# Mamba-2 scan and maxout FFN on one core: first decay exponents by matmul, one early load of the decays, loads reordered, two weight tiles decoded inside the first scan

## The chip, the cores and the metric

The kernel runs on one core of a Trainium2 chip. The metric is the device time of one execution in microseconds (us). "Span" below is the profiled length of an execution, some 1.6 to 3 us shorter than its time. "Granted clock" is the share of full speed at which the trace shows TensorE's clock running. The profile views write PE for TensorE, DVE for VectorE, ACT for ScalarE, POOL for GpSimd and SP for SyncE; PEld is TensorE loading weights, and a q behind a name is an engine's queue, here issuing loads.

## The reference

The first half is a state-space scan (4 batches, 8 heads, 768 tokens, head size 32, state size 16). The second half is a maxout feed-forward layer over the 3072 tokens. Cut to what matters:

```python
log_a = np.log(np.clip(a, 1e-06, 1.0))
for c in range(nc):                                   # blocks of tokens
    cum = np.cumsum(log_a[:, :, sl], axis=-1)
    L = np.exp(cum[:, :, :, None] - cum[:, :, None, :]) * causal
    M = np.einsum('bhin,bhjn->bhij', Cc, Bc) * L
    y = M @ xc + (Cc @ state) * np.exp(cum)           # written in short
    decay_from_j = np.exp(cum[:, :, -1:] - cum)
    state = ...                                       # (cut) uses decay_from_j
# then, with x = y as (3072, 256); the weights are float64
h = np.maximum(np.maximum(x @ w1, x @ w2), x @ w3)    # 256 -> 768
out = h @ w_out                                       # 768 -> 256
```

## The kernel before

The kernel works on six blocks of 128 tokens of all four batches (the reference's chunks are 32, the result is the same). While TensorE runs the feed-forward layer of one block (`up` for the six groups f of 128 hidden columns, then `down`), the other engines prepare the scan of the next. Block 0 has no block before it to hide behind: its scan and the decoding of the weights are laid bare.

The weights arrive as pairs of 32-bit words and have to be turned into fp32: 12 tiles, nine of w1 to w3 and three of w_out. The n-th call of `decode` starts the n-th tile and finishes the one before; calls 10 to 12 start the w_out tiles, and call 13 only finishes. In the views below, `rb` is a raw weight tile, `w_u` and `w_r` are steps of its decoding, `w` and `wo` the decoded tiles; `spread` and `L` hold the decay exponents and then their exps, `s` the scan's scores, `y` and `yT` its output; `m` and `h` are the running and the final maximum of a group f, `o` is the output of `down`.

```python
def first():                      # first step of a decode
    nc.scalar.activation(u, hi, AF.Abs)                       # ScalarE
    nc.vector.tensor_scalar(u, u, SMALL, LARGE, max, min)     # VectorE, "clamp"
    nc.vector.tensor_scalar(u, u, 3, logical_shift_left)      # VectorE, "shift"
    nc.scalar.activation(r, lo, AF.Copy, ...)                 # ScalarE
    nc.gpsimd.tensor_tensor(out=r, in0=u, in1=r, op=ALU.add)  # GpSimd
def second():                     # finish: the tile is usable after this
    nc.vector.scalar_tensor_tensor(out=dst, in0=hi, ..., in1=r)   # VectorE
# ... (arguments shortened)
lg0 = logs(cum0, "lg0")                       # first scan starts
for c in range(NC):                           # six small loads, on ScalarE
    w, k = divmod(c, NC // 2)
    nc.scalar.dma_start(out=a_sb[k * BH:(k + 1) * BH, w],
                        in_=a_rows[:, c * P:(c + 1) * P])
# ... (cut) exponents of block 0: L[j, i] = cum[i] - cum[j] + mask, then exp
scan_bd(0)                                    # Bd = B * decay_from_j, GpSimd
s01 = scan_scores(0, 0)
scan_weights(0, 0, s01)
decode()
# ... (cut)
for _ in range(6):
    fetch()                                   # weight tiles
decay_load(1)                                 # L of block 1
last_load(1)                                  # E of block 1
load(1, "B"); load(1, "C"); load(1, "x")
while weight_jobs:
    fetch()                                   # w_out comes last
scan_out(0, ffn_bank)
decode(); decode(); decode()
# fillers: one is run after each third of an up
fillers += 7 * [decode] + decays_of(1) + 4 * [decode]
# after the first f: transposes for block 1, then A = Bd^T x of block 0
```

## Time and profile before

The first record of the kernel before is 333.13 us (three runs). I follow five milestones of block 0 on the timeline.

| milestone (profile before) | us from the span's start |
|---|---|
| first `up` starts | 34.50 |
| `up` of f=1 starts | 44.92 |
| GpSimd starts the first select of block 1's decays | 61.10 |
| VectorE starts the last maximum (h) of block 0 | 79.52 |
| end of the span | 332.3 |

The select is a milestone because 32 exps of ScalarE, the scan inputs of block 1 and the last decodes stand behind it in order. The last h is one because the rest of the run follows it at a fixed distance: 332.3 - 79.52 = 252.8 us.

These are two lines of TensorE's timeline and two of VectorE's before the change. The columns are start, duration, engine, line, operation, output and inputs, sizes, count, and in brackets how long the engine had stood and what released it.

```profile
57.12 1.98 PE L472 MATMUL up<-yT,w 128*128 128x512 f32 x4 [0.24 <-ACT m L477]
60.67 3.70 PE L472 MATMUL up<-yT,w 128*128 128x512 f32 x8 [1.57 <-DVE m L479]
...
78.50 1.09 DVE L166 SCALAR_TENSOR_TENSOR wo<-rb,w_r 128x512 uint32<-128x512 uint32 x1 [0.57 <-POOL w_r L163]
79.52 0.68 DVE L479 TENSOR_TENSOR h<-m,up 128x512 f32<-128x512 f32 x1
```

They show that the stretch ends with the last w_out tile (`wo`, finished at 79.6) and the last h. TensorE's own waits in it are short.

### The profile page before, as it was taken

To read this page: it belongs to the slowest core of one execution; us is meant where nothing else is said; L and a number is where in the kernel's file an instruction comes from. 1 tells how busy PE (TensorE), PEld (TensorE's weight loads), DVE (VectorE), ACT (ScalarE), POOL (GpSimd) and SP (SyncE) were. 2 spreads that over 40 slices of the span, in tenths; PEclk is the share of its full clock that TensorE was granted. 3 is DMA by queue.
4 is the path that set the end of the run, shared out by engine and by line. 5 is a ranking of instruction groups with operands and counts; after the bars stand their busy time and mean duration, and the time that the engine had idled before them with its cause. 6 is when DMAs were issued, how large, how long until landed. Compare 5 with 4: busy or idle time off the path is not lost.

```text
span 332.3 us, 4455 instructions
## 1 busy us (share of the span) xinstructions
PE 306.4 (92%) x1734; PEld 176.3 (53%) x1734; DVE 119.6 (36%) x198; ACT 111.7 (34%) x275; POOL 54.6 (16%) x59
## 2 busy tenths in 40 slices
PE   2188879899999999999999999999999999999995
PEld 2165334346754446845447845447845448644474
DVE  1178977545312354013334013423023433032210
ACT  1074725592456017433025433134423101101100
POOL 5001554805400025000033000050000000000000
PEclk9999779999999999999999999999999999999999
DMA  8908979790048700068600177600000000000001
GB/s 84 251 2 293 368 85 292 251 116 3 34 147 206 90 2 1 34 210 160 76 0 0 34 263 107 73 0 2 34 33 0 0 0 34 34 0 0 0 1 63
DMA packets 87333, 28.07 MB, mean 84 GB/s; under 512 B 75536, under 2 KB 81680, under 8 KB 87312
## 3 DMA queue, kind: packets, MB, share of 16 engines
q1 hardware_dynamic: 86928, 27.66, 36.8%
q8 instruction: 13, 0.21, 0.2%
q10 hardware_dynamic: 384, 0.13, 0.2%
q14 instruction: 8, 0.07, 0.1%
HBM read 24.54 MB, written 3.24 MB: 84 GB/s over the span
## 4 chain that ended last, share of the span: by engine, by line
PE 80%; ACT 5%; DVE 5%; DMA 4%; issue 2%; SPq 2%; POOL 1%; ACTq 0%; POOLq 0%; DVEq 0%
PE up L472 48%; PE o L489 19%; PE s L420 5%; PE y L450 4%; ACT L L342 3%; DMA raw_x<-in_x_dram 2%; DVE w_u L154 2%; DMA rb<-in_moe_w_out_dram 2%; PE y L442 2%; DVE w L166 1%; PE trC L363 1%; PE spread L289 1%; ACT w_u L153 1%; SPq L101 1%; SPq L137 1%
## 5 line engine op out<-in xcount | busy, mean ns | idle before, releaser
L472 PE MATMUL up<-yT,w 128*128 128x512 f32 x432 | 193.2, 603 | 6.0 <-ACT w_r L162 2.7
L472 PEld LDWEIGHTS up<-yT,w 128*128 128x128 f32 x432 | 81.9, 193 | 104.9 <-issue 92.9
L489 PE MATMUL o<-wo,h 128*128 128x256 f32 x288 | 65.4, 384 | 0.1
L479 DVE TENSOR_TENSOR m<-m,up 128x512 f32<-128x512 f32 x36 | 24.7, 687 | 102.2 <-PE up L472 73.9
L489 PEld LDWEIGHTS o<-wo,h 128*128 128x128 f32 x288 | 53.8, 190 | 10.4 <-issue 2.8
L477 ACT COPY m<-up 128x512 f32<-128x512 f32 x36 | 21.0, 584 | 109.9 <-PE up L472 109.9
L342 ACT ACTIVATE L<-L,ncums 128x128 f32<-128x128 f32 x160 | 48.5, 391 | 10.1 <-POOL L L338 10.1
L479 DVE TENSOR_TENSOR h<-m,up 128x512 f32<-128x512 f32 x36 | 24.7, 687 | 29.1 <-PE up L472 28.8
L429 DVE TENSOR_TENSOR L<-s,L 128x512 f32<-128x512 f32 x48 | 29.8, 683 | 8.7 <-PE s L420 8.7
L163 POOL TENSOR_TENSOR w_r<-w_u,w_r 128x512 uint32<-128x512 uint32 x12 | 18.5, 1540 | 37.8 <-DVE w_u L157 35.3
L493 ACT COPY ob<-o 128x512 f32<-128x512 f32 x12 | 7.0, 583 | 48.1 <-PE o L489 40.0
L338 POOL TENSOR_SCALAR_AFFINE_SELECT L<-L 128x1024 f32<-128x1024 f32 x20 | 21.2, 1092 | 0.0
L420 PE MATMUL s<-CT,BT 32*128 32x256 f32 x192 | 17.6, 446 | 1.4 <-ACT CT L374 1.4
L420 PEld LDWEIGHTS s<-CT,BT 32*128 32x128 f32 x192 | 11.4, 206 | 10.4 <-issue 6.4
L406 POOL TENSOR_TENSOR old<-S,E 128x256 f32<-128x256 f32 x4 | 2.5, 620 | 73.7 <-issue 73.7
L455 DVE COPY yT<-y 128x512 f32<-128x512 f32 x6 | 4.2, 692 | 25.5 <-PE y L450 25.5
L450 PE MATMUL y<-L,raw_x 128*32 128x128 f32 x384 | 12.4, 285 | 0.0
L154 DVE TENSOR_SCALAR w_u<-w_u 128x512 f32<-128x512 f32 x12 | 10.6, 885 | 4.8 <-ACT w_u L153 4.7
L450 PEld LDWEIGHTS y<-L,raw_x 128*32 128x32 f32 x384 | 10.7, 115 | 1.6 <-issue 1.5
L409 POOL TENSOR_TENSOR S<-S,old 128x256 f32<-128x256 f32 x4 | 2.9, 724 | 47.6 <-DVE S L401 47.6
L153 ACT ACTIVATE w_u<-rb 128x512 f32<-128x512 f32 x12 | 8.1, 679 | 4.1 <-DMA rb<-in_moe_w_out_dram 4.1
L455 ACT COPY yT<-y 128x512 f32<-128x512 f32 x6 | 3.5, 585 | 17.0 <-PE y L450 17.0
(60 smaller groups left out, 112.8 us busy)
## 6 DMA issues: line engine op xcount, KB each, us to landing
L<-cums SPq DMA_DIRECT2D x20, 512.0 KB, 7.0
rb<-in_moe_w_dram SPq DMA_DIRECT2D x9, 512.0 KB, 6.8
raw_x<-in_x_dram SPq DMA_DIRECT2D x6, 512.0 KB, 7.3
out_dram<-ob SPq DMA_DIRECT2D x12, 256.0 KB, 2.2
raw_B<-in_B_dram SPq DMA_DIRECT2D x6, 256.0 KB, 4.4
raw_C<-in_C_dram SPq DMA_DIRECT2D x6, 256.0 KB, 6.3
rb<-in_moe_w_out_dram SPq DMA_DIRECT2D x3, 512.0 KB, 5.8
E<-cums SPq DMA_DIRECT2D x40, 32.0 KB, 5.9
```

Of the source, the lines that this page charges most:

```text
L153: nc.scalar.activation(u.bitcast(FP32), hi.bitcast(FP32), AF.Abs)
L154: nc.vector.tensor_scalar(out=u.bitcast(FP32), in0=u.bitcast(FP32), scalar1=SMALL, scalar2=LARGE, op0=ALU.max, op1=ALU.min)
L163: nc.gpsimd.tensor_tensor(out=r, in0=u, in1=r, op=ALU.add)
L338: nc.gpsimd.affine_select(out=L[:, b], in_=L[:, b], pattern=[[0, NH], [1, P]], compare_op=ALU.is_ge, fill=MASKED, base=0, channel_multipli ...
L342: nc.scalar.activation(L[:, b, h], L[:, b, h], AF.Exp, bias=ncum[c][:, b * NH + h:b * NH + h + 1], scale=1.0)
L420: nc.tensor.matmul(out=banks[r][:, i].rearrange("j g i -> j (g i)"), lhsT=st["BT"][rows, b], rhs=st["CT"][rows, b].rearrange("p g i -> p ( ...
L429: nc.vector.tensor_tensor(out=M, in0=banks[r], in1=M, op=ALU.mult)
L450: nc.tensor.matmul(out=ys[t][q * D:(q + 1) * D, b], lhsT=st["x"][:, b * NH + h], rhs=M[:, b, h], start=(c == 0 and b == 0), stop=True, til ...
L472: nc.tensor.matmul(out=p, lhsT=w_sb[i][:, k, f * P:(f + 1) * P], rhs=yT[c][:, k], start=(k == 0), stop=(k == KD - 1))
L477: nc.scalar.copy(out=m, in_=p)
L479: nc.vector.tensor_tensor(out=m if i == 1 else hT[c][:, f], in0=m, in1=p, op=ALU.max)
L489: nc.tensor.matmul(out=o[:, i], lhsT=hT[c][:, f, b * P:(b + 1) * P], rhs=wo_sb[:, f], start=(f == 0), stop=(f == NF - 1), skip_group_check ...
```

## The change

The intent is to start TensorE's steady work earlier. One load of all of `a` goes out before ScalarE's table load. The exponents of batches 0 and 1 are built wholly in PSUM by matmul, so ScalarE can take their exp directly. Two weight tiles are decoded between the steps of the first scan. Loads are fewer and in another order, and `Bd` of block 0 moves behind the first f.

```diff
+    a_sb = const.tile([R, 2, P], FP32, name="a_sb")
+    nc.scalar.dma_start(out=a_sb, in_=...)          # all of a, one load
     tabs = list(get_activation_tables(nc.m.arch).keys())
...
-    for c in range(NC):                             # the six late loads
-        nc.scalar.dma_start(...)
...
+    def spread_mask(b):                             # mask into PSUM
+        for g in range(2):
+            nc.tensor.matmul(out=spread[b, g], lhsT=ident, rhs=mask..., start=True, stop=False)
+    def spread_j(bs):                               # minus cum[j] into PSUM
+            nc.tensor.matmul(out=spread[b, g], lhsT=cum0[rows, 0], rhs=npick..., start=False, stop=True)
...
-    cums = dram.tile([NC, BH, P], FP32, name="cums")
+    cums = dram.tile([BH, NC, P], FP32, name="cums")
-        for b in range(NB):                         # L: 4 loads of 512 KB
+        for b in range(0, NB, 2):                   # L: 2 loads of 1 MB
...
-    scan_bd(0)
-    s01 = scan_scores(0, 0)
-    scan_weights(0, 0, s01)
     decode()
-    s23 = scan_scores(0, 2)
-    scan_weights(0, 2, s23)
+    scan_weights(0, 0, scan_scores(0, 0))
+    decode()
+    scan_weights(0, 2, scan_scores(0, 2))
     fj = from_last(R, a_sb, "fj")
-    for _ in range(6):
+    for _ in range(3):
         fetch()
     decay_load(1)
-    last_load(1)
+    for _ in range(3):
+        fetch()
     load(1, "B")
     load(1, "C")
+    last_load(1)
     load(1, "x")
     while weight_jobs:
         fetch()
+    decode()
     scan_out(0, ffn_bank)
-    decode()
-    decode()
     decode()
...
     def first_tokens():                             # behind the first f
+        from_j[0] = by_token(BH, fj0, "from_j0", 1.0)[:, :, 0]
+        scan_bd(0)
...
-    fillers += 7 * [decode] + decays_of(1) + 4 * [decode]
+    fillers += 6 * [decode] + decays_of(1) + 3 * [decode]
```

(Arguments are shortened and cuts are marked by dots.)

More of the change, by code (lines that the diff above doesn't have):

```diff
@@ L83 @@
         eng.dma_start(out=a0[k * BH:(k + 1) * BH], in_=a_rows[:, 0:P])
+    a_sb = const.tile([R, 2, P], FP32, name="a_sb")
+    nc.scalar.dma_start(
+        out=a_sb,
+        in_=a_rows.rearrange("r (c i) -> (r c) i", i=P).rearrange("(w r) i -> r w i", w=2))
     tabs = list(get_activation_tables(nc.m.arch).keys())
@@ L196 @@
         out=pick, in_=ident.rearrange("p (r k) -> p k r", k=BH), op=ALU.add, axis=AX.X)
+    npick = const.tile([P, BH], FP32, name="npick")
+    nc.vector.tensor_scalar(
+        out=npick, in0=pick, scalar1=-1.0, scalar2=None, op0=ALU.mult)
     hsel = const.tile([HN, NH], FP32, name="hsel")
@@ L247, in by_token @@
                 out=tp[:, w], in_=src[0:rows, w], identity=ident[0:rows, 0:rows])
-        t = const.tile([P, n * rows // BH, BH], FP32, name=name)
+        t = const.tile([P, BH, n * rows // BH], FP32, name=name)
         nc.vector.tensor_scalar(
-            out=t.rearrange("p c k -> p (c k)"), in0=tp.rearrange("p w r -> p (w r)"),
+            out=t.rearrange("p k c -> p (k c)"), in0=tp.rearrange("p w r -> p (w r)"),
             scalar1=scale, scalar2=None, op0=ALU.mult)
         return t
-    ncum, from_j = {}, {}
-    cum0 = a0.unsqueeze(1)
-    clip(cum0)
-    lg0 = logs(cum0, "lg0")
-    a_sb = const.tile([R, 2, P], FP32, name="a_sb")
-    for c in range(NC):
-        w, k = divmod(c, NC // 2)
-        nc.scalar.dma_start(
-            out=a_sb[k * BH:(k + 1) * BH, w], in_=a_rows[:, c * P:(c + 1) * P])
-    running(P, lg0, cum0)
-    ncum[0] = by_token(BH, cum0, "ncum0", -1.0)[:, 0]
-    fj0 = from_last(BH, cum0, "fj0")
     Ls = {}
@@ L274, in decays, with spread_banks, row_tile, spread_i @@
         return Ls[c]
-    L0 = decays(0)
-    spread = {}
-    def spread_first(b0):
-        for i in range(2):
-            for g in range(2):
-                spread[b0 + i, g] = att_bank([P, HALF, P], "spread")
-        for k in range(HALF):
-            for i in range(2):
-                for g in range(2):
-                    rows = slice((2 * i + g) * BH, (2 * i + g + 1) * BH)
-                    n = (b0 + i) * NH + g * HALF + k
-                    nc.tensor.matmul(
-                        out=spread[b0 + i, g][:, k],
-                        lhsT=pick[rows, n:n + 1].to_broadcast([BH, P]), rhs=cum0[rows, 0],
-                        start=(k == 0), stop=True, tile_position=((2 * i + g) * BH, 0),
-                        skip_group_check=True)
+    def spread_banks(b, banks):
+        for g, bank in enumerate(banks):
+            spread[b, g] = bank([P, HALF, P], "spread")
+    def spread_mask(b):
+        for g in range(2):
+            nc.tensor.matmul(
+                out=spread[b, g].rearrange("p k i -> p (k i)"), lhsT=ident,
+                rhs=mask.unsqueeze(1).to_broadcast([P, HALF, P]), start=True, stop=False,
+                skip_group_check=True)
+    def row_tile(b, g):
+        r = (2 * b + g) % REP * BH
+        return slice(r, r + BH), (r, 0)
+    def spread_i(bs, start):
+        for k in range(HALF):
+            for b in bs:
+                for g in range(2):
+                    rows, pos = row_tile(b, g)
+                    n = b * NH + g * HALF + k
+                    nc.tensor.matmul(
+                        out=spread[b, g][:, k],
+                        lhsT=pick[rows, n:n + 1].to_broadcast([BH, P]), rhs=cum0[rows, 0],
+                        start=(start and k == 0), stop=start, tile_position=pos,
+                        skip_group_check=True)
+    def spread_j(bs):
+        for b in bs:
+            for g in range(2):
+                rows, pos = row_tile(b, g)
+                n = b * NH + g * HALF
+                nc.tensor.matmul(
+                    out=spread[b, g].rearrange("p k i -> p (k i)"), lhsT=cum0[rows, 0],
+                    rhs=npick[rows, n:n + HALF].unsqueeze(2).to_broadcast([BH, HALF, P]),
+                    start=False, stop=True, tile_position=pos, skip_group_check=True)
     def below(b):
@@ L300, in below, with first_sums, first_exps @@
             channel_multiplier=-1)
-    def first_sums(b, filled):
+    def first_sums(b):
         for g in range(2):
             part = L0[:, b, g * HALF:(g + 1) * HALF]
-            if filled:
-                nc.vector.tensor_tensor(
-                    out=part, in0=spread[b, g], in1=part, op=ALU.add)
-            else:
-                for k in range(HALF):
-                    n = b * NH + g * HALF + k
-                    nc.vector.scalar_tensor_tensor(
-                        out=part[:, k], in0=spread[b, g][:, k], scalar=ncum[0][:, n:n + 1],
-                        in1=mask, op0=ALU.add, op1=ALU.add)
-    def first_exps(b):
+            nc.vector.tensor_tensor(out=part, in0=spread[b, g], in1=part, op=ALU.add)
+    def first_exps(b, summed):
         for g in range(2):
             part = L0[:, b, g * HALF:(g + 1) * HALF]
-            nc.scalar.activation(part, part, AF.Exp)
-    cums = dram.tile([NC, BH, P], FP32, name="cums")
+            nc.scalar.activation(part, part if summed else spread[b, g], AF.Exp)
+    ncum, from_j = {}, {}
+    L0, spread = decays(0), {}
+    for b in range(2):
+        spread_banks(b, 2 * [att_bank])
+        spread_mask(b)
+    cum0 = a0.unsqueeze(1)
+    clip(cum0)
+    lg0 = logs(cum0, "lg0")
+    running(P, lg0, cum0)
+    ncum[0] = by_token(BH, cum0, "ncum0", -1.0)[:, :, 0]
+    cums = dram.tile([BH, NC, P], FP32, name="cums")
     def decay_load(c):
         L = decays(c)
-        for b in range(NB):
+        for b in range(0, NB, 2):
             nc.sync.dma_start(
-                out=L[:, b], in_=cums[c, b * NH:(b + 1) * NH, :].partition_broadcast(P))
+                out=L[:, b:b + 2].rearrange("j b h i -> j (b h) i"),
+                in_=cums[b * NH:(b + 2) * NH, c, :].partition_broadcast(P))
     def last_load(c):
         E = blocks[c]["E"] = raw.tile([HN, NB, P], FP32, tag="E", name="E")
-        rows = cums[c].rearrange("(b h) s -> h b s", h=NH)
+        rows = cums[:, c].rearrange("(b h) s -> h b s", h=NH)
         for h in range(NH):
@@ L496, in down @@
             in_=ob)
-    spread_first(0)
-    from_j[0] = by_token(BH, fj0, "from_j0", 1.0)[:, 0]
-    for b in range(1, NB):
+    for b in range(2, NB):
         below(b)
-    first_sums(0, False)
-    first_exps(0)
+    spread_i((0, 1), False)
+    spread_j((0, 1))
+    spread_banks(2, (att_bank, ffn_bank))
+    spread_i((2,), True)
+    first_exps(0, False)
+    fj0 = from_last(BH, cum0, "fj0")
     scan_b(0, ffn_bank)
-    spread_first(2)
-    first_sums(1, True)
-    first_exps(1)
+    first_sums(2)
     clip(a_sb)
-    first_sums(2, True)
+    first_exps(1, False)
+    spread_banks(3, (att_bank, att_bank))
+    spread_i((3,), True)
+    lg = logs(a_sb, "lg")
     scan_c(0, ffn_bank)
-    lg = logs(a_sb, "lg")
-    first_sums(3, True)
-    first_exps(2)
-    first_exps(3)
     running(R, lg, a_sb)
+    first_exps(2, True)
+    first_sums(3)
     nc.sync.dma_start(
-        out=cums.rearrange("c k s -> (c k) s").rearrange("(w r) s -> r w s", w=2), in_=a_sb)
-    scan_bd(0)
-    s01 = scan_scores(0, 0)
-    scan_weights(0, 0, s01)
+        out=cums.rearrange("k c s -> (k c) s").rearrange("(w r) s -> r w s", w=2), in_=a_sb)
+    first_exps(3, True)
     decode()
-    s23 = scan_scores(0, 2)
-    scan_weights(0, 2, s23)
+    scan_weights(0, 0, scan_scores(0, 0))
+    decode()
+    scan_weights(0, 2, scan_scores(0, 2))
     fj = from_last(R, a_sb, "fj")
-    for _ in range(6):
+    for _ in range(3):
         fetch()
     decay_load(1)
-    last_load(1)
+    for _ in range(3):
+        fetch()
     load(1, "B")
     load(1, "C")
+    last_load(1)
     load(1, "x")
@@ L549, in first_tokens @@
         from_js = by_token(R, fj, "from_js", 1.0)
+        from_j[0] = by_token(BH, fj0, "from_j0", 1.0)[:, :, 0]
+        scan_bd(0)
         for c in range(1, NC):
-            ncum[c], from_j[c] = ncums[:, c], from_js[:, c]
+            ncum[c], from_j[c] = ncums[:, :, c], from_js[:, :, c]
         scan_state(0)
     pieces = [(up, f) for f in range(NF)] + [(down, u) for u in range(NB // 2)]
-    fillers += 7 * [decode] + decays_of(1) + 4 * [decode]
+    fillers += 6 * [decode] + decays_of(1) + 3 * [decode]
     for c in range(NC):
```

## The prediction

> **What bounds the kernel now.** I read the page's busy shares and 40 slices, then the chain that ended last, then the timeline of the first 90 us engine by engine.
>
> ```profile
> PE 306.4 (92%) x1734; PEld 176.3 (53%) x1734; DVE 119.6 (36%) x198; ACT 111.7 (34%) x275; POOL 54.6 (16%) x59
> ...
> PE   2188879899999999999999999999999999999995
> ```
>
> TensorE is busy 92%, and from the twelfth slice on (8.3 us each) it is always full. From 88.35 us the chain holds almost only TensorE, one block of 128 tokens every 48.6 us (`up` begins at 93.73, 142.30, 190.88). The change leaves that part alone. So only the first 88 us can shorten, and a microsecond won there counts only if it is still won when the first block's `down` runs. From the first `up`, steady TensorE work is six blocks of 36 x 0.858 + 48 x 0.224 = 41.7 us and five scans of about 6.5 us: 282 us; with 3.6 us of tail, a start at 34.5 would end at 320. The kernel ends at 332.3, so some 12 us are lost after the first `up`; the rest of what can be won lies before it.
>
> ScalarE's timeline shows the first hole:
>
> ```profile
> 3.67 0.31 ACT L225 ACTIVATE lg<-a 128x128 f32<-128x128 f32 x1 [0.67 <-DVE a L220]
> 3.68 11.15 ACTq L263 DMA_DIRECT2D a_sb<-in_a_dram  x6
> 14.88 0.40 ACT L238 ACTIVATE fj<-a 32x128 f32<-32x128 f32 x1 [10.89 <-DMA raw_x<-in_x_dram]
> ```
>
> ScalarE issues six loads of `a`. The last of them waits for a semaphore that the load of x holds until 14.5. So `fj` starts at 14.88, its transpose at 15.33, and what stands behind it in the order of TensorE and VectorE later still.
>
> The second stretch is the first block's `up`, with the weights being decoded beside it (timeline, all engines):
>
> ```profile
> 33.90 1.60 POOL L163 TENSOR_TENSOR w_r<-w_u,w_r 128x512 uint32<-128x512 uint32 x1 [3.98 <-DVE w_u L157]
> 34.27 1.51 DVE L154 TENSOR_SCALAR w_u<-w_u 128x512 f32<-128x512 f32 x1
> 34.50 6.90 PE L472 MATMUL up<-yT,w 128*128 128x512 f32 x12 [2.67 <-ACT w_r L162]
> ...
> 44.92 11.95 PE L472 MATMUL up<-yT,w 128*128 128x512 f32 x24 [1.51 <-DVE h L479]
> ...
> 55.36 0.66 ACT L153 ACTIVATE w_u<-rb 128x512 f32<-128x512 f32 x1 [4.13 <-DMA rb<-in_moe_w_out_dram]
> ...
> 61.10 3.18 POOL L338 TENSOR_SCALAR_AFFINE_SELECT L<-L 128x1024 f32<-128x1024 f32 x3
> ```
>
> y is ready at 32.6, but the first weight tile only at 34.4. Then each decoded tile costs a loop of GpSimd 1.57, VectorE's blocked clamp about 0.3, shift 0.43 and a handover: 2.46 us from one GpSimd add to the next (36.38, 38.88, 41.36). The maxima wait in VectorE's order behind these, so the second f starts only at 44.92. At 51.2 ScalarE stands 4.13 us for a w_out tile, which holds up the copy of f=2 and costs TensorE 0.24 + 1.57 us at 57 to 61.
>
> **What the Trainium skill says.** "DMA: Bandwidth & Descriptors", section "Anatomy of one DMA": a semaphore wait of a DMA happens on the issuing sequencer before dispatch. The trace agrees: ScalarE stood 10.89 us for loads that it only issued. "SBUF — State Buffer", section "Who interferes with whom": VectorE in a two-port mode and GpSimd take the shared ports as an exclusive lock, the second blocks. The trace agrees: the clamp takes 0.43 us alone and 1.51 beside GpSimd's add. "TensorE: Matmul & The Clock Gate", Part 1: half clock until an activity window of some 3.4 us was busy. The trace agrees: granted clock 0.50 at 35 to 37 us, 1.00 from 38, a 512-column pass taking 0.86 us and then 0.43. At 45 to 47 it was 0.50 again. The same DMA page, "Specifications": pieces of 512 B or more go at line rate. The loads of L change from 4 KB pieces to 512 B ones; no view of this trace settles that.
>
> **The change part by part.**
>
> (a) One early load of `a` removes the 11 us stand of ScalarE. It costs one issue, about 0.4 us as the others, ahead of the table load.
>
> (b) The exponents of batches 0 and 1 are made by matmul. Removed: one GpSimd select (1.09 us), eight small VectorE sums (2.15) and two large ones (1.28). Added: four mask matmuls, 8 passes of 512 columns, and four 32-row ones. The mask is ready at 2.44. From 2.55 about 2.7 us run cold: 3.2 passes at 0.86, then 4.8 at 0.43, end near 7.6 (9.4 if the clock stays low). Sixteen spreads and the four 32-row matmuls, four at a time in the array: about 1.1 and 1.0 us. The exponents are complete near 10.3, and ScalarE starts there.
>
> (c) ScalarE from 10.3: exps 1.2, fj 0.4, BT 0.5, exps 1.15, log 0.4, CT 1.2, exps 2.2, first decode step 0.66: 18.0. VectorE follows: clamp and shift 0.9, weights of batches 0 and 1 2.48 (the row of L429), second clamp and shift 0.9, finish of tile 0 0.7, weights 2.48, clamp and shift 0.9, finish of tile 1 0.7, yT 0.7: 27.8 us. Tile 0 and tile 1 are there, so the first `up` starts near **28**, against 34.5: **6.5 us won**.
>
> (d) from_j moves behind the first f. Now TensorE's f=1 stands behind A, A behind Bd on GpSimd, Bd behind the seventh decode's add and behind from_j on VectorE. From the start of `up`: copy of m at 3.5, decode 5 clamps at 4.75, GpSimd adds until 7.3, 9.75 and 12.2 (period 2.46), Bd 1.06 until 13.3, A 0.65: f=1 starts 14.05 us after the first, not 10.45. **3.6 us lost**: 42.0 against 44.92. TensorE is idle some 6.5 us and starts cold, as before.
>
> (e) From f=1 the pattern of before repeats (m copied after 3.4 us; decodes 8 to 10), but without the stand for w_out: that tile should land near 44 to 47 (before: 31 us after `cums` was sent; now sent near 15), and decode 10 reads it near 48. The select for block 1 starts near 54 instead of 61.1. **4 us won back**: 6.9 ahead there.
>
> (f) Decode 11 moves from before that select to just ahead of the score weights of block 1. ScalarE: 32 exps of 0.305, two copies 0.94, BT, CT, E 2.1, decode step 0.66: 13.5 us from 55.1: 68.6. VectorE then: decode 11 1.5, weights 2.5, decode 12 1.6, maximum 0.65, wait and finish of the last tile 2, last h 0.7: 77. Before, that h ended at 80.2 (the weights ran before decode 12 had its data). **3.6 us lost again**; 3.2 us remain. TensorE, done with `up` by 71.5, waits here for tiles and h; its clock may drop, for up to 1.3 us in `down`.
>
> (g) Half as many loads of L, and E behind B and C: hidden, these loads have slack.
>
> Sum: 6.5 - 3.6 + 4.0 - 3.6 - 0.5 for the clock = 2.8 us. 333.1 - 2.8 = **330.3**; I take 330.
>
> **The rivals.** First: everything won at the start survives, because the losses in (d) and (f) are smaller (from_j or Bd earlier, ScalarE's work packed closer). Then 6.5 us or more remain: 326.5 or less. For it: 12 us of loss after the first `up`, and two of the waits named go. Against it: both new places stand in the engines' fixed order. Second: the mask matmuls stay at half clock (end 9.4, spreads 2.1, the last 1.9): the exponents come at 13.7, 3.4 us later, all passed on: 333. For it: TensorE was slow in 15 to 30 us (a transpose 277 ns, later 110), though the clock row reads 1.00 there. Against it: dense work warmed it after 2.8 us at 34.5 and at 44.9. Third: the 512 B pieces slow the loads, and w_out arrives after 48; each microsecond then delays the select: 331 to 334.
>
> **Range and chances.** The first rival sets the low end, 325.8, the second and third the high end, 332.9. Faster by over 2% needs under 326.5, which is nearly the whole start kept: 0.15. Slower by over 2% needs 7 us of new loss: 0.02. Within 2%: 0.83.
>
> **What would show it.** Right: no ScalarE stand before 10 us; exponents at 10 to 11.5; first `up` at 27 to 30; a TensorE gap of 6 to 7 us ahead of f=1, ended by Bd and A; no long stand for w_out; VectorE doing decode 11 ahead of the block-1 weights, and TensorE waiting for h and wo at 72 to 77; then the unchanged 48.6 us period. Wrong: if f=1 follows the first f within 4 us, or `down` starts straight after A, the gain is 6 us or more; if the mask matmuls end after 9, or ScalarE stands for w_out, it is nil.

## The result, and the profile after

The changed kernel takes 329.3 us (median of four runs, 328.71 to 330.51) against 333.37 us (333.1 to 334.7). Ratios here are the mean time of one kernel's fast runs over that of the other's of the same rounds, so they are not quite the ratio of the medians: 0.9875, with a 95% interval of 0.9836 to 0.9913. It is faster, by less than 2%. All outputs are right. The medians differ by 4.1 us and the two profiled spans by 5.0: the profiled run of the kernel before was one of its slower ones (334.03 us), and both kernels' runs scatter by 1.6 to 1.8 us.

| milestone | before | after | lead, predicted | lead, measured |
|---|---|---|---|---|
| first `up` | 34.50 | 26.31 | 6.5 | 8.2 |
| `up` of f=1 | 44.92 | 39.46 | 2.9 | 5.5 |
| select of block 1 | 61.10 | 52.32 | 6.9 | 8.8 |
| last h of block 0 | 79.52 | 74.50 | 3.3 | 5.0 |
| end of span | 332.3 | 327.3 | 2.8 (time) | 5.0 |

The predicted lead is the running sum of the prediction's terms (its text has 3.2 at the last h, read from its times).

The page of the changed kernel, busy time per engine and the 40 slices of TensorE and of its granted clock:

```profile
PE 307.3 (94%) x1750; PEld 175.7 (54%) x1750; DVE 113.3 (35%) x189; ACT 111.4 (34%) x275; POOL 54.1 (17%) x58
...
PE   6868399988999999999999999999999999999995
...
PEclk9959699999999999999999999999999999999999
```

TensorE's work is the same (307.3 us against 306.4), but it begins sooner: the first slice (8.2 us) is six tenths busy instead of two. The dip to 3 in the fifth slice is the gap ahead of f=1, and the granted clock falls there too. The two 8s in the ninth and tenth slice (65 to 82 us) are new waits in `down`. ScalarE's timeline after:

```profile
1.72 0.45 ACTq L86 DMA_DIRECT2D a_sb<-in_a_dram  x1
...
10.73 1.09 ACT L324 ACTIVATE L<-spread 128x512 f32<-128x512 f32 x2 [6.83 <-PE spread L304]
...
49.03 0.68 ACT L158 ACTIVATE w_u<-rb 128x512 f32<-128x512 f32 x1 [3.60 <-DMA rb<-in_moe_w_out_dram]
```

The stand of 10.89 us has gone: the load takes 0.45 us to issue, and ScalarE now waits for TensorE's exponents, which it has at 10.7. The stand for w_out is still there, 3.60 us instead of 4.13. TensorE's timeline after:

```profile
2.50 6.19 PE L276 MATMUL spread<-mask,ident 128*128 128x512 f32 x8 [2.50 <-POOL mask L220]
...
26.31 5.42 PE L491 MATMUL up<-yT,w 128*128 128x512 f32 x12 [0.47 <-ACT yT L474]
...
38.45 1.08 PE L413 MATMUL A<-raw_x,Bd 128*32 128x64 f32 x32 [3.77 <-POOL Bd L403]
39.46 16.80 PE L491 MATMUL up<-yT,w 128*128 128x512 f32 x36
...
71.92 1.13 PE L508 MATMUL o<-wo,h 128*128 128x256 f32 x4 [0.86 <-DVE wo L171]
74.64 3.89 PE L508 MATMUL o<-wo,h 128*128 128x256 f32 x16 [1.58 <-DVE wo L171]
```

The first `up` no longer waits for a weight tile but for y itself. Ahead of f=1 TensorE waits for `A`, and `A` for `Bd`. In `down` (the rows of `o`) it now waits twice for w_out tiles; before, the 24 passes of the first half of `down` took 5.99 us from 77.54, and the same passes in the second half, without a wait, 5.45. GpSimd's and VectorE's timelines show what they wait for:

```profile
35.83 1.55 POOL L168 TENSOR_TENSOR w_r<-w_u,w_r 128x512 uint32<-128x512 uint32 x1 [0.92 <-DVE w_u L162]
37.34 1.05 POOL L403 TENSOR_TENSOR Bd<-raw_B,from_j 128x512 f32<-128x512 f32 x1
...
52.32 3.17 POOL L357 TENSOR_SCALAR_AFFINE_SELECT L<-L 128x1024 f32<-128x1024 f32 x3
```

```profile
67.40 0.69 DVE L171 SCALAR_TENSOR_TENSOR wo<-rb,w_r 128x512 uint32<-128x512 uint32 x1
68.00 2.48 DVE L448 TENSOR_TENSOR L<-s,L 128x512 f32<-128x512 f32 x4
...
73.03 1.55 DVE L171 SCALAR_TENSOR_TENSOR wo<-rb,w_r 128x512 uint32<-128x512 uint32 x1 [0.56 <-POOL w_r L168]
74.50 0.67 DVE L498 TENSOR_TENSOR h<-m,up 128x512 f32<-128x512 f32 x1
```

`Bd` stands right behind a decode's add, and the last decodes and the last h stand behind the score weights of block 1 (2.48 us). From the last h to the end it is 252.8 us, as before.

### The profile page after: what moved, and what is told of

The parts are those of the page before. It is cut to its first block, busy times and chain, and to the rows that moved or that the text cites. A ratio compares the mean times of both kernels' runs of the same rounds, so it can differ in the third digit from the quotient of the medians.

```text
span 327.3 us, 4457 instructions
## 1 busy us (share of the span) xinstructions
PE 307.3 (94%) x1750; PEld 175.7 (54%) x1750; DVE 113.3 (35%) x189; ACT 111.4 (34%) x275; POOL 54.1 (17%) x58
## 4 chain that ended last, share of the span: by engine, by line
PE 79%; SPq 6%; ACT 5%; DMA 4%; DVE 2%; issue 1%; POOL 1%; POOLq 0%; ACTq 0%; DVEq 0%
PE up L491 48%; PE o L508 19%; PE s L439 3%; PE y L469 3%; ACT L L361 3%; SPq L106 2%; PE spread L276 2%; DMA rb<-in_moe_w_out_dram 2%; PE y L461 2%; SPq L142 1%; SPq L352 1%; DMA cums<-a_sb 1%; SPq L344 1%; DMA E<-cums 1%; DVE L L448 1%
## 5 line engine op out<-in xcount | busy, mean ns | idle before, releaser
L491 PE MATMUL up<-yT,w 128*128 128x512 f32 x432 | 190.9, 597 | 0.9 <-ACT yT L474 0.5
L439 PE MATMUL s<-CT,BT 32*128 32x256 f32 x192 | 16.3, 421 | 4.0 <-DVE L L448 2.6
L439 PEld LDWEIGHTS s<-CT,BT 32*128 32x128 f32 x192 | 10.6, 193 | 12.3 <-issue 6.4
L159 DVE TENSOR_SCALAR w_u<-w_u 128x512 f32<-128x512 f32 x12 | 7.2, 604 | 9.0 <-ACT w_u L158 9.0
```

Source lines behind the costliest of these rows:

```text
L439: nc.tensor.matmul(out=banks[r][:, i].rearrange("j g i -> j (g i)"), lhsT=st["BT"][rows, b], rhs=st["CT"][rows, b].rearrange("p g i -> p ( ...
L491: nc.tensor.matmul(out=p, lhsT=w_sb[i][:, k, f * P:(f + 1) * P], rhs=yT[c][:, k], start=(k == 0), stop=(k == KD - 1))
```

## The experiments

All twelve were timed in three rounds, four experiments in each; those of one round ran on the same chip and share the runs of the kernel before (the groups are named below the table). All milestones and spans are from the one profiled run of each kernel. "Rest" is span minus start of the last h.

| kernel | first `up` | f=1 | select | last h | span | rest | median time | ratio (95%) |
|---|---|---|---|---|---|---|---|---|
| before | 34.50 | 44.92 | 61.10 | 79.52 | 332.3 | 252.8 | 333.37 | 1 |
| after | 26.31 | 39.46 | 52.32 | 74.50 | 327.3 | 252.8 | 329.3 | 0.9875 (0.9836 to 0.9913) |
| e1_bd_early | 26.89 | 34.98 | 52.80 | 75.00 | 327.8 | 252.8 | 328.77 | 0.9876 (0.984 to 0.9912) |
| e2_wout_early | 26.27 | 39.41 | 51.21 | 73.40 | 326.2 | 252.8 | 329.21 | 0.9879 (0.986 to 0.9897) |
| e3_bd_wout | 26.01 | 34.05 | 44.82 | 67.00 | 321.4 | 254.4 | 323.2 | 0.9713 (0.9687 to 0.9739) |
| e4_load_alone | 27.79 | 38.38 | 52.90 | 71.32 | 324.2 | 252.9 | 325.84 | 0.9785 (0.9769 to 0.9801) |
| e5_sums_back | 25.24 | 38.26 | 51.72 | 73.92 | 326.7 | 252.8 | 328.84 | 0.9863 (0.982 to 0.9905) |
| e6_pieces_8k | 26.13 | 39.29 | 51.81 | 73.99 | 328.5 | 254.5 | 328.86 | 0.9858 (0.9818 to 0.9898) |
| e9_d11_back | 25.86 | 39.00 | 54.45 | 73.33 | 326.2 | 252.9 | 328.25 | 0.984 (0.9805 to 0.9874) |
| e7_bd_wout_d11 | 26.89 | 34.97 | 48.19 | 67.06 | 319.9 | 252.8 | 322.06 | 0.9646 (0.9602 to 0.9691) |
| e8_mask_bf16 | 24.07 | 32.20 | 47.11 | 65.99 | 318.8 | 252.8 | 319.04 | 0.9586 (0.9558 to 0.9614) |
| e10_three_sums | 25.17 | 33.00 | 46.22 | 65.10 | 318.2 | 253.1 | 319.99 | 0.9604 (0.9588 to 0.962) |
| e11_bf16_pieces | 25.44 | 33.58 | 48.50 | 67.39 | 320.3 | 252.9 | 322.87 | 0.9678 (0.9638 to 0.9719) |
| e12_load_wout | 27.58 | 38.16 | 52.98 | 71.41 | 324.3 | 252.9 | 325.7 | 0.9766 (0.9745 to 0.9788) |

The medians of the kernel before were 333.14 (beside e1 to e4), 333.33 (e5, e6, e7, e9) and 333.45 (e8, e10, e11, e12).

The rest of 252.8 us in ten of the twelve experiments, within 0.3, is the check on the whole method: in the profiled runs of these ten, whatever happens in the first 80 us reaches the end through the last h of block 0. The two exceptions are described under e3.

### e1: Bd back in the first scan

The theory is that f=1 starts late because `A` waits for `Bd`. The rival is that the decode chain, not `Bd`, sets the start of f=1.

```diff
     first_sums(3)
+    from_j[0] = by_token(BH, fj0, "from_j0", 1.0)[:, :, 0]
+    scan_bd(0)
...
     def first_tokens():
-        from_j[0] = by_token(BH, fj0, "from_j0", 1.0)[:, :, 0]
-        scan_bd(0)
```

> The changed kernel with from_j of block 0 and its product Bd made during the first scan, as the kernel before had it, and nothing else. Theory (two waits in a row: A waits for Bd, and later ScalarE waits for the w_out tile that lands at 49 us whatever the compute does): the gap of TensorE between f=0 and f=1 (31.7 to 39.5 us) shrinks by 4 to 5 us, but ScalarE's stand for w_out grows from 3.6 us to 8 or 9, the select of block 1 stays at 52 us, and the end moves by less than 1 us. Rival (the Bd gap is the loss that counts): the end comes 4 to 5 us earlier.

The timelines of TensorE, ScalarE and GpSimd in e1:

```profile
34.98 1.98 PE L491 MATMUL up<-yT,w 128*128 128x512 f32 x4 [1.51 <-DVE h L498]
...
49.54 0.66 ACT L158 ACTIVATE w_u<-rb 128x512 f32<-128x512 f32 x1 [9.65 <-DMA rb<-in_moe_w_out_dram]
...
52.80 3.19 POOL L357 TENSOR_SCALAR_AFFINE_SELECT L<-L 128x1024 f32<-128x1024 f32 x3
```

f=1 starts 8.1 us after the first `up` instead of 13.15, and waits for the h of the first f. So `Bd` was the cause of the gap. But the span is 327.8, not shorter (the medians, 328.77 and 329.3, differ by less than the scatter). ScalarE simply stands longer for w_out (9.65 us instead of 3.60), which lands at the same time, and the select comes at 52.80. The 4.5 us won at f=1 are all handed to the next wait.

### e2: w_out sent before block 1's inputs

```diff
+    while weight_jobs:
+        fetch()
     load(1, "B")
     load(1, "C")
     last_load(1)
     load(1, "x")
-    while weight_jobs:
-        fetch()
```

> The changed kernel with the three w_out tiles fetched ahead of B, C, E and x of block 1, and nothing else. Theory (the w_out landing sets the select of block 1): the w_out stand of ScalarE (3.6 us) vanishes, the select starts near 48.7 instead of 52.3, the last h of the first block near 71 instead of 74.5, and the kernel ends 3 to 3.6 us earlier (ratio to the kernel before about 0.977). Rival (the select could have come earlier without use, because the end hangs on TensorE's start of f=1): no change, within 0.7 us.

VectorE's and GpSimd's timelines in e2:

```profile
48.16 0.90 DVE L159 TENSOR_SCALAR w_u<-w_u 128x512 f32<-128x512 f32 x1
...
49.70 1.56 POOL L168 TENSOR_TENSOR w_r<-w_u,w_r 128x512 uint32<-128x512 uint32 x1 [0.92 <-DVE w_u L162]
...
51.21 3.18 POOL L357 TENSOR_SCALAR_AFFINE_SELECT L<-L 128x1024 f32<-128x1024 f32 x3
```

The stand of 3.60 us is gone, but the select comes only 1.1 us earlier. GpSimd's adds now follow one another at 44.73, 47.22 and 49.70: once f=1 has begun, the decode period of 2.48 us sets the select. The stand was worth 1.1 us in the profile, and nothing that the times can show (0.9879 against 0.9875). The expected 48.7 for the select and 3 us at the end were misses.

### e3: both

> Both edits: Bd in the first scan and w_out ahead of B, C, E and x. Theory (the two waits hide one another): far more than the sum of the two alone; f=1 starts near 34.5, select near 43, last h near 66 to 68, end 7 to 9 us earlier than the changed kernel (ratio to the kernel before about 0.963). Rival (independent losses): the sum of the two single gains, about 3.5 to 4 us.

The diff is that of e1 and e2 together. GpSimd's and TensorE's timelines:

```profile
44.82 3.18 POOL L357 TENSOR_SCALAR_AFFINE_SELECT L<-L 128x1024 f32<-128x1024 f32 x3
...
67.14 5.41 PE L508 MATMUL o<-wo,h 128*128 128x256 f32 x16 [1.58 <-DVE wo L171]
```

The select comes at 44.82, 7.5 us earlier, where e1 and e2 alone brought -0.5 and 1.1. The two waits lie side by side, each hiding the other, and only taking both away shows their worth. The span falls by 5.9 us. It would fall by 7.5, but the last 16 passes of `down` take 5.41 us instead of 3.89: after the wait of 1.58 us for a w_out tile the granted clock was 0.72 in the stretch from 68 to 73 us. The changed kernel has the same wait before the same passes and its clock there was 1.00; e6 has it too and went cold (5.47 us). e2 and e5 have it too (1.59 us) and stayed warm. So whether that wait costs another 1.5 us is not decided by the wait's length. What decides it these runs do not show.

### e4: the early load alone, on the kernel before

```diff
+    a_sb = const.tile([R, 2, P], FP32, name="a_sb")
+    for k in range(NC // 2):
+        nc.scalar.dma_start(out=a_sb[k * BH:(k + 1) * BH],
+                            in_=a_rows.rearrange("r (w k i) -> k r w i", w=2, i=P)[k])
     tabs = list(get_activation_tables(nc.m.arch).keys())
...
-    for c in range(NC):
-        w, k = divmod(c, NC // 2)
-        nc.scalar.dma_start(...)
```

(Three loads instead of one, because the kernel before keeps `a` in the older order of rows. They are all ahead of the table load.)

> The kernel before with one part of the change alone: its six late loads of a replaced by three at the start, ahead of the activation table load. Theory (the 11 us stand of ScalarE was the whole of what the start lost): the stand vanishes, fj runs near 4.5 us, the first up starts near 26 to 28 us as in the changed kernel, and at least 4 us of the span are won, as much as by the whole change. Rival (the exponents by matmul are what makes the start short): the first up starts no earlier than 30 us, and the gain is under 2 us.

ScalarE's and TensorE's timelines in e4:

```profile
1.74 1.97 ACTq L87 DMA_DIRECT2D a_sb<-in_a_dram  x3
...
5.84 0.40 ACT L244 ACTIVATE fj<-a 32x128 f32<-32x128 f32 x1 [0.49 <-DVE a L236]
...
27.79 7.25 PE L473 MATMUL up<-yT,w 128*128 128x512 f32 x12 [2.45 <-DVE w L172]
```

The load costs 1.97 us of issue, `fj` starts at 5.84 instead of 14.88, and the span is 324.2: 8.1 us shorter than before (7.3 between the medians of the times) and 3.1 shorter than that of the whole change. The intervals of the two ratios (0.9769 to 0.9801, and 0.9836 to 0.9913) do not touch, and e12, which has the same load on another chip, agrees (0.9766). So this one edit won more than the whole change, and the rest of the change, taken together, lost about 3 us. (Whether e4 is faster than the kernel before by 2% or more is unclear: the interval ends at 0.9801.) The first `up` in e4 still waits 2.45 us for its weight tile, as in the kernel before.

### e5: the old exponents back

In the changed kernel, batches 0 and 1 get their exponents as before (spread by matmul, then sums on VectorE); everything else stays.

```diff
-        spread_mask(b)
...
-    spread_i((0, 1), False)
-    spread_j((0, 1))
+    spread_i((0, 1), True)
+    first_sums_stt(0)          # eight small VectorE sums, as before
+    first_sums(1)
```

> The changed kernel with the exponents of batches 0 and 1 made as before (VectorE's eight small sums for batch 0, GpSimd's select and two large sums for batch 1; no mask and no 32-row matmuls), all else of the change kept. Theory (the single early load is what shortened the start; the matmul exponents save VectorE 3.4 us but hold TensorE for 6 us at half clock): the first up starts within 1.5 us of the changed kernel's 26.3, the end moves by less than 2 us either way. Rival (the matmul exponents carry the start): the first up starts at 28.5 us or later and the end is over 2 us later.

The first `up` starts 1.1 us earlier with the old sums (25.24 against 26.31), and the span is 0.6 us shorter. The times overlap. So making the exponents wholly by matmul brings nothing: the slow mask passes occupy TensorE until 8.7, while the old way began to spread at 4.61.

### e6: loads of L in 8 KB pieces

The changed kernel again with `cums` as [NC, BH, P], so that the pieces of one load of L are 8 KB long and not 512 B; the load of `a` becomes three loads as in e4.

```diff
-    cums = dram.tile([BH, NC, P], FP32, name="cums")
+    cums = dram.tile([NC, BH, P], FP32, name="cums")
...
-                in_=cums[b * NH:(b + 2) * NH, c, :].partition_broadcast(P))
+                in_=cums[c, b * NH:(b + 2) * NH, :].partition_broadcast(P))
```

> The changed kernel with the running sums stored by block again, so that each of the two loads of L has pieces of 8 KB instead of 512 B (the load of a becomes three, one for each piece of the order). Theory (512 B pieces move at 290 GB/s where 4 KB pieces moved at 400 to 410): the L loads move at 380 GB/s or more, w_out lands 2 to 3 us earlier, ScalarE's stand shrinks from 3.6 us to about 1.5, but VectorE's decodes then set the select (51.2 us as in the run with w_out early), so the end moves by 1 us at most. Rival (the pieces do not matter): the rate stays near 290 GB/s and w_out lands at 49.

First the windows view of the changed kernel, then that of e6, while the loads of L run. The columns are the window, its length, busy time of TensorE, weight loads, VectorE, ScalarE and GpSimd, granted clock, DMA share and GB/s.

```profile
22.00:24.00 2.00, 2.00 (x31) 1.29 (x32) 2.00 (x4) 0.00 (x0) 1.59 (x1) 0.50 1.20 300
24.00:26.00 2.00, 1.84 (x44) 1.33 (x36) 1.97 (x5) 0.33 (x1) 0.12 (x1) 0.85 1.22 291
```

```profile
22.00:24.00 2.00, 2.00 (x41) 1.85 (x42) 2.00 (x4) 0.00 (x0) 1.06 (x1) 0.50 1.03 427
24.00:26.00 2.00, 1.87 (x32) 1.28 (x24) 1.77 (x5) 0.51 (x2) 0.74 (x1) 0.50 0.96 396
```

The 512 B pieces move some 295 GB/s, the 8 KB ones some 410. w_out is read at 47.15 instead of 49.03. But the select comes only 0.5 us earlier, for the reason seen in e2, and the time does not change beyond its scatter. The slower pieces are real, and no cost of them shows at the end here.

### e9: decode 11 back ahead of the select

```diff
-    fillers += 6 * [decode] + decays_of(1) + 3 * [decode]
+    fillers += 7 * [decode] + decays_of(1) + 2 * [decode]
```

> The changed kernel with seven decodes ahead of the decays of block 1 and two behind, as in the kernel before, in place of six and three: decode 11 goes back ahead of the select. Nothing else. Theory (in its new place decode 11 costs about 3 us: it stands ahead of the score weights while down waits for the last tile and h): the select starts later, near 54.8 instead of 52.3, but the last h of the first block ends near 73.3 instead of 75.2 and the kernel ends about 2 us earlier (ratio to the kernel before about 0.981). Rival (the later select costs what the later weights save): no change within 0.7 us.

From the select to the last h it is 18.9 us instead of 22.2, as in the kernel before (18.4): 3.3 us won there. The select itself comes 2.1 us later (54.45 against 52.32), since one more decode precedes it. The last h starts 1.2 us earlier. The times lean the same way but their intervals overlap.

### e7: e1, e2 and e9 together

> The three edits together: Bd in the first scan, w_out ahead of B, C, E and x, decode 11 ahead of the select. Theory: the select moves from 44.8 (the two edits without the third) to about 47.3, the last h from 67.7 to about 65.8, the end 1.5 to 2 us earlier than with the two (span near 319.7, ratio to the kernel before about 0.966). Rival (with the waits gone the order of decode 11 no longer matters, TensorE sets the end): no change against the two edits.

The span is 319.9, which is 7.4 us under the changed kernel. One by one the three edits gave -0.5, 1.1 and 1.1 us in spans (0.5, 0.1 and 1.1 in medians). Against e3 the last h is no earlier (67.06, where 65.8 was expected), but TensorE's wait in `down` is 0.57 us instead of 1.58, the 16 passes take 3.89 us, and the rest is back at 252.8.

That the last h is no earlier does not mean that the order of decode 11 paid nothing, because the two profiled runs started differently. These are TensorE's mask matmuls in e3, then in e7:

```profile
2.55 5.38 PE L276 MATMUL spread<-mask,ident 128*128 128x512 f32 x8 [2.55 <-POOL mask L220]
```

```profile
2.50 6.71 PE L276 MATMUL spread<-mask,ident 128*128 128x512 f32 x8 [2.50 <-POOL mask L220]
```

Up to here the two kernels do the same, yet the mask ends at 7.93 in one and 9.21 in the other. In the seven profiled kernels with this mask its end lies between 7.93 and 9.21 us, and the first `up` between 25.86 and 26.89, the latest where the mask ends latest (e1 and e7). So a single profiled start is uncertain by about 1 us. From f=1 to the last h, e7 takes 32.1 us and e3 33.0: the order seems to have won some 0.9 us, which the later start took back.

### e12: the kernel before with the early load and w_out sent early

> The kernel before with two edits alone: the early loads of a, and w_out fetched right behind the L loads. None of the rest of the change. Theory (w_out still holds ScalarE for 3.9 us after the early load alone, though VectorE's decodes need most of that time): the stand vanishes, the select starts 1.5 to 2.5 us earlier than 52.9, the end 1 to 2.5 us earlier than the early load alone (324.2 us of span), so two moved loads win 9 to 10 us. Rival (VectorE's decodes take the place of the wait at once): under 0.7 us.

This is e4 with the w_out loads right behind the loads of L. The select comes at 52.98 against 52.90, the span is 324.3 against 324.2. So with the order of the kernel before, the stand for w_out is worth nothing at all.

### e10: e7 with the old exponents

> The three edits together, with the exponents of batches 0 and 1 made as before the change, by VectorE and GpSimd. Theory (the matmul exponents are no gain even when the later waits are gone): the first up starts 1 us or so earlier than with them (25.2 against 26.3 us in the single comparison), and the end is 0 to 1.5 us earlier than with the three edits. Rival (they pay once the later waits no longer hide it): the end is 1 us or more later.

The span is 318.2, which is 1.7 us under e7, and the time 319.99. e7 and e10 ran on different chips, and the intervals of their ratios overlap a little (0.9602 to 0.962). It agrees with e5: the matmul exponents, with this mask, do not pay. (Some of the 1.7 us is e7's late start, described above; e10 starts without the mask.) e10 is also to be read against e12, which ran beside it. Both have the early load, w_out sent early, `Bd` in the first scan, decode 11 ahead of the select and the old exponents. What e10 has besides is the rest of the change: two tiles decoded between the steps of the first scan, the first scan's own order, the order and pieces of the loads, and one load of `a` in place of three (ScalarE's first logarithm starts at 3.52 instead of 5.05). It is worth 324.3 - 318.2 = 6.1 us (5.7 between the medians of the times). These four were not separated further. That the decoded tiles are the main cause is only read from the traces. These are the first `up` of e12 and that of e10:

```profile
27.58 7.08 PE L473 MATMUL up<-yT,w 128*128 128x512 f32 x12 [2.67 <-ACT w_r L168]
```

```profile
25.17 5.42 PE L499 MATMUL up<-yT,w 128*128 128x512 f32 x12 [0.26 <-ACT yT L482]
```

TensorE stands 2.67 us for a decode in e12, and 0.26 us for y in e10.

### e8: e7 with the mask in bf16

```diff
+    ident_h = const.tile([P, P], BF16, name="ident_h")
+    nc.vector.tensor_copy(out=ident_h, in_=ident)
+    mask_h = const.tile([P, P], BF16, name="mask_h")
+    nc.vector.tensor_copy(out=mask_h, in_=mask)
...
-                out=spread[b, g]..., lhsT=ident, rhs=mask...
+                out=spread[b, g]..., lhsT=ident_h, rhs=mask_h...
```

> The three edits together (Bd early, w_out early, decode 11 ahead of the select) and the mask matmuls on bf16 copies of mask and identity, which hold their values to within rounding that the exponential does not see. Theory (the mask matmuls are in the way for their 6.2 us of slow passes): they end near 5 instead of 8.6 us, the exponents are complete 1.5 to 2 us earlier, and the end is 1 to 2 us earlier than with the three edits alone (319.9 us of span). Rival (ScalarE and VectorE set the first scan, or the first f waits for B and C): under 0.5 us.

TensorE's timeline in e8:

```profile
2.75 1.87 PE L281 MATMUL spread<-mask_h,ident_h 128*128 128x512 bf16 x4 [2.75 <-DVE mask_h L227]
...
24.07 5.42 PE L496 MATMUL up<-yT,w 128*128 128x512 f32 x12 [0.47 <-ACT yT L479]
```

The mask takes 1.87 us instead of 6.19: four passes instead of eight, each at half the time. TensorE is still slow then: the 32 spreads behind the mask take 2.17 us, and 1.21 in the changed kernel. The first `up` starts at 24.07, the earliest of all, and the median is 319.04 us, the lowest of all. In the profiles 2.8 us are won on e7 at the first `up` but only 1.1 at the last h (65.99 against 67.06), because in this run TensorE was slow again after its wait of 1.51 us ahead of f=1: the granted clock was 0.50 from 33 to 35 us, and ScalarE copies the first result of f=1 3.7 us after its start, in e7, after the same wait, 2.0 us after. The profiled run was e8's slowest; the spans of the other three are 316.7 to 317.1. e10's runs (319.84 to 320.28) lie within the range of e8's (318.79 to 320.87), so which of the two is better is not settled. Both beat the kernel before by about 4% and the changed kernel by about 3%.

### e11: e8 with the 8 KB pieces of e6

> The three edits, the bf16 mask and the 8 KB pieces of L together. Theory: with w_out already early, the faster L loads move nothing on the path; the end is within 1 us of the run with the three edits and the bf16 mask, and the L loads move at 390 GB/s or more. Rival (tiles of weights 3 to 8 still wait for these loads): 1 us or more earlier.

The time is 322.87, no gain over e8 and by the intervals a loss (0.9638 to 0.9719 against 0.9558 to 0.9614). The three issues of the load of `a` hold up ScalarE's logarithm, so the first transpose on TensorE comes at 5.87 instead of 4.55, and the first `up` at 25.44. Faster pieces do not earn that back. That explains 1.4 us, the difference of the two profiles at the select and at the last h (both went slow at f=1); the rest of the 3.8 us between the medians is open.

## Why the prediction was right or wrong

The time (329.3 us against 330.0), faster by less than 2%, came out as predicted. The steps behind it did so only in part, and some of the agreement is luck: the lead was 4.1 us in medians and 5.0 in the profiled spans, against 2.8 in the sum, and of its terms (c), (d) and the clock were too pessimistic by 1.7, 0.9 and 0.5 us, (e) and (f) too optimistic by 0.7 and 0.2.

**Step (a), the early load: right, and larger than its place in the sum.** ScalarE's stand is gone. e4 shows that it alone is worth 8.1 us at the end. I had folded its worth into the step up to the first `up`. (e4 issues three loads where the change issues one.)

**Step (b), the exponents: right in the end, wrong on the clock and on the worth.** I put the end of the mask at 7.6 (my own pass times give 7.4), or 9.4 if the clock stayed low; it was 8.7, and from 7.93 to 9.21 over the seven kernels with this mask. The first passes started about 0.85 us apart until 7.7, about 5.2 us after the first, where I had taken 2.7 us. Exponents were ready at 10.7 (I had 10.3). That this way of making them is a gain, e5 and e10 do not show; with the shorter bf16 mask of e8 it is level with the old way.

**Step (c), the first `up`: mechanism right, size off.** It started at 26.31, not 28. VectorE's row of work was as listed (weights 2.48 us twice, decodes between), and `up` now waits for y alone. It began at 17.87 (I had 18.0) and reached its own half of the copy of y at 26.25, where my durations give 27.1: the pieces overlap by about 0.1 us each. And the first pass of `up` needs only ScalarE's half of that copy; the 0.7 us of VectorE's half, which I had added, lies beside it.

**Step (d), Bd behind the first f: right.** f=1 started 13.15 us after the first `up` (predicted 14.05), behind `A`, behind `Bd`, behind a decode's add. The loss was 2.7 us instead of 3.6. (The decode period that I read as 2.46 us is 2.48 to 2.50 between the adds that I quote.) e1 shows that `Bd` caused it, and that it cost nothing at the end by itself, since w_out came late anyway. That last point I had not seen.

**Step (e) is the one that failed: "but without the stand for w_out".** I had w_out landing near 44 to 47 and read at 48. It was read at 49.03 after a stand of 3.60 us. Two things went otherwise. `cums` was sent at 14.87 as I had taken it, but w_out was read 34.2 us later, not 31. With 8 KB pieces (e6) it was read 32.9 us after `cums`, so the slower pieces account for some 1.3 of these 3 us; the rest was not separated. And the decode came to it sooner. Still the lead grew by 3.3 us there, close to my 4.0, for another reason: one decode fewer stands ahead of the select, which e9 puts at 2.1 us. The stand that I had priced at 4 us was worth 1.1 (e2) or nothing (e12), because the decode period of 2.48 us on VectorE and GpSimd took its place at once; only with `Bd` out of the way (e3 against e1) did its removal bring the select 8.0 us forward. So the term came out right by the work moved in step (f), not by the cause I gave it. A stand for w_out was also among my signs that the gain would be nil; it came, and the gain was not nil.

**Step (f), decode 11 behind the score weights: right.** From the select to the last h it was 22.2 us against 18.4, a loss of 3.8 (predicted 3.6; VectorE's row as I listed it ends at 77.55 and not at 77, which would make it 4.2), and e9 wins 3.3 of it back. But e9 also shows that the same move is what gained 2.1 us in step (e): its net cost is 1.2 us at the last h of the profiled runs, not 3.6, and the times do not separate even that from nothing.

**Term (g), the clock, and "hidden" loads.** I took 0.5 us for TensorE cooling in `down`. In the profiled run it was 0. In e3 and e6 it was 1.5 us. A share of the scatter of the changed kernel (328.71 to 330.51, the slowest at a mean clock of 0.967 instead of 0.979) may be that; no trace of that run shows it. The loads that I called hidden had little slack: ScalarE stood 0.34 us for a weight tile in the changed kernel, 1.14 in e7 and 2.48 in e8. No cost of these stands is shown.

**The rivals.** The first, that the whole start survives, was wrong for the change as it is: of 8.2 us won, 5.0 remained in the profile. It was right about what could be had, since e3, e7, e8 and e10 keep the start and come to 318 to 321 us of span. The second, a mask at half clock, was half true: it ended between my two cases. The third, slow 512 B pieces, was true of the rate and wrong on the cost: e6 moves the select by 0.5 us only.

**The account.** In spans, the early load gives -8.1 (e4). The rest of the first scan's order, with two tiles decoded in it, gives -6.1 (e10 against e12). The exponents by matmul cost +1.7 (e7 against e10). `Bd`, w_out and decode 11 where the change put them cost +7.4 (after against e7). The sum is -5.1, and the measured difference -5.0. That they agree proves nothing: the parts are differences along one chain of kernels (before, e4, e12, e10, e7, after), so they must add up but for the step from e4 to e12, which is 0.1. What each step holds besides its name was not always separated (e10 against e12). The parts come from runs on three chips, and the spans of the kernel before alone range from 331.1 to 333.5, so differences under a microsecond should not be leaned on.

## What to carry to other kernels

A wait that the trace shows at its full length is worth only what is left when the next wait ends: here taking away 4.5 us at f=1 or a stand of 3.6 us gave nothing or 1.1 at the select, and taking away both gave 7.5. When a start has been won, follow it milestone by milestone to the last instruction that the steady part hangs on, and ask at each which other engine or load arrives next. And try the parts of a change alone: here its smallest edit, loading `a` early, won more than the whole.

## What the Trainium skill lacked or had wrong

- "DMA: Bandwidth & Descriptors", section "Specifications", has line rate from 512 B on. Loads of L in 512 B pieces moved 291 to 300 GB/s, while the same bytes in 8 KB pieces moved 396 to 427, and the 4 KB ones of the kernel before 411 from 34 to 38 us. For this broadcast from DRAM to SBUF, 512 B is not line rate.
- "TensorE: Matmul & The Clock Gate", Part 1, puts the warm-up near 3.4 us of sustained work and calls the moment run-variable. At the start of the changed kernel dense fp32 passes stayed slow for 5.2 us (starts 0.74 to 1.01 us apart from 2.50 to 7.7), while the granted clock in the trace read 1.00. There the clock row cannot be read as warm; pass durations tell. In seven kernels the same eight passes ended anywhere from 7.93 to 9.21.
- The same Part 1 has the clock fall after an idle window of about 3.4 us. In e3 and e6 a wait of 1.58 us in `down` was followed by cold passes (16 of them in 5.41 and 5.47 us); after the same wait in the changed kernel they took 3.89. In e8 and e11 the clock fell to 0.50 after a wait of 1.51 and 1.52 us ahead of f=1, in e7 (1.51 us) it did not. So a shorter wait can be followed by a low clock, and the page gives no length for that.
- No page that I read has what a small load can cost the engine that issues it when the issue has to wait for another load: in the kernel before, the last of six loads of `a` kept ScalarE standing for 10.89 us, until the load of x, issued by SyncE, had landed.
